# Sparse attention into two MLPs on one core: two batches divide P ahead of its transposing and multiply with V of both heads as the stationary operand

## The chip, the core and the metric

The kernel runs on one core of a Trainium2 chip. The metric is the device time of one execution in microseconds (us). Engines: PE (TensorE), DVE (VectorE), ACT (ScalarE), POOL (GpSimd), and SP, which here only issues DMAs. Each engine works through its own queue in program order; semaphores tie the queues together.

## The reference

Attention over 4 batches, 8 heads, 576 positions and 64 dimensions in float32. The first four heads see the last 32 positions (local), the last four see the earlier positions with the same remainder by 32 (strided). Then two MLPs of 2304 tokens, each 512 to 2048 to 512 with a squared relu.

```python
scores = np.where(masks, scale * (q @ k.T), -1e9)
attn = np.exp(scores - scores.max(-1))
attn = attn / (attn.sum(-1) + 1e-09)
x = (attn @ v)                       # heads side by side: 2304 x 512
for w_in, w_out in ((moe_w_in, moe_w_out), (moe2_w_in, moe2_w_out)):
    h = np.maximum(x @ w_in, 0.0)
    x = (h * h) @ w_out
```

## The kernel before

**The MLPs.** Weights and activations are split into a high and a low fp32r part, and each product is three matmuls. Layer 0 runs over five blocks of tokens (512, 512, 512, 256, 512), each block in steps of 128 hidden rows. In step s the program issues mm1(s+1) (12 matmuls into ps_h; L704), then a relu and a square on ACT (r L744, gh L752) and two DVE products (sq L753, gl L754) on its result, then mm2(s) (12 matmuls into ps_y; L757).

**The attention.** x, the input of layer 0, comes from attention in 48 fills, 12 for each batch. A fill takes two heads u: three local ones for u = 0 (96 queries and 128 keys in each of two groups), three for u = 1, then three strided ones for each u (blocks of 126 in two groups, of 108 in two groups, of 108 in one). Fills are numbered 0 to 47; batch 3 has 24 to 35, batch 4 has 36 to 47. Batches 1 and 2 have their own orders (`ALONE`, `SHARED`), and batches 3 and 4 the order `BETWEEN` (L625).

**A fill in batches 3 and 4.** split_qk (L325: ACT and DVE split queries and keys, and SP loads the next ones), scores_first and scores_second (L351, a head each), mask_first and mask_second (L379, L381: mask and minimum on DVE), exponent (L484, four ACT instructions, in place in s), turn_p (L491, PE transposes of P into ps_pt), keep_p (L499, ACT copies it to pt), values (L507: P is stationary, V with a column of ones moves, so that the sum of P comes out as column 65), divide (L538, L539, L541: DVE adds 1e-9, takes the reciprocal and multiplies into xn), turn_x (L553, PE transposes of xn into ps_x), keep_x (L592, ACT writes the high part of x) and rest_x (L596, DVE writes the low part).

**The order.** `BETWEEN` has ten slots. An entry (function, back) in round n works on fill n - back; all slots are laid end to end in one list `att`. The MLP calls point() after each three matmuls, eight points a step; points 1 to 3 lie inside mm1, point 4 behind it and behind the issue of r, gh, sq and gl, points 5 to 7 inside mm2, point 8 behind it. At each point `att_to` issues as many slots as are due: batch 3 is spread evenly over points 8 of step 15 to 4 of step 30 (116 points), batch 4 over the same stretch 16 steps on. Values are not issued at once: they are put in a list `small`, of which one comes out behind each MLP matmul; divide, in the same slot, issues all that are left.

**Buffers.** The PSUM ring ps_a has three banks, which scores, ps_pt, ps_o and ps_x of batches 3 and 4 take in turn. ps_h has one bank. s, m, pt and den have two buffers each, v has five.

Of the kernel before, what the change touches and what calls it, by code (L numbers as in the profile page):

```python
# [9 lines left out]
F32 = mybir.dt.float32  # L10
F32R = mybir.dt.float32r
I32 = mybir.dt.int32
AF = mybir.ActivationFunctionType
ALU = mybir.AluOpType
AX = mybir.AxisListType

P = 128
B, H, S, D = 4, 8, 576, 64
STRIDE = 32
NPOS = S // STRIDE  # L20
# [6 lines left out]
BLOCKS = [  # L27
    [(0, TB), (TB, TB), (2 * TB, TB), (3 * TB, TB // 2), (NT - TB, TB)],
    [(0, TB // 2)] + [(n * TB + TB // 2, TB) for n in range(4)],
]  # L30
# [21 lines left out]
FIRST_2 = 2  # L52


SFILLS = [(0, 7, 2), (14, 6, 2), (26, 6, 1)]
LQ, LK = 2 * QB, 2 * QB + STRIDE
# [28 lines left out]
def pack_local(q, k, v):  # L85


    qk = np.zeros((B, 2, 3, P, 2 * LQ + LK), np.float32)
    ov = np.ones((B, 2, 3, P, 2, 2, D + 1), np.float32)
    kp = np.zeros((B, 4, STRIDE + S, D), np.float32)  # L90
    vp = np.zeros((B, 4, STRIDE + S, D), np.float32)
    kp[:, :, STRIDE:] = k[:, :4]
    vp[:, :, STRIDE:] = v[:, :4]
    for u in range(2):
        for f in range(3):
            for h in range(2):
                n, rows = 2 * u + h, slice(h * D, (h + 1) * D)
                qk[:, u, f, rows, h * LQ:(h + 1) * LQ] = q[:, n, f * LQ:(f + 1) * LQ].transpose(0, 2, 1)
                qk[:, u, f, rows, 2 * LQ:] = kp[:, n, f * LQ:f * LQ + LK].transpose(0, 2, 1)
                for g in range(2):  # L100
                    k0 = f * LQ + g * QB
                    ov[:, u, f, :, h, g, :D] = vp[:, n, k0:k0 + P]
    return qk, ov.reshape(B, 2, 3, P, VW)


def pack_strided(q, k, v, fill):

    r0, n, ng = fill
    m = n * NPOS
    w = ng * m  # L110
    qk = np.zeros((B, 2, P, 3 * w), np.float32)
    ov = np.ones((B, 2, P, 2, ng, D + 1), np.float32)

    def rows_of(x):
        x = x[:, 4:].reshape(B, 4, NPOS, STRIDE, D)[:, :, :, r0:r0 + n * ng]
        return x.transpose(0, 1, 3, 2, 4).reshape(B, 4, w, D)

    qq, kk, vv = rows_of(q), rows_of(k), rows_of(v)
    for u in range(2):
        for h in range(2):  # L120
            rows = slice(h * D, (h + 1) * D)
            qk[:, u, rows, h * w:(h + 1) * w] = qq[:, 2 * u + h].transpose(0, 2, 1)
            qk[:, u, rows, 2 * w:] = kk[:, 2 * u + h].transpose(0, 2, 1)
            for g in range(ng):
                ov[:, u, :m, h, g, :D] = vv[:, 2 * u + h, g * m:(g + 1) * m]
    return qk, ov.reshape(B, 2, P, 2 * ng * (D + 1))


def both_halves(qk, w, groups):


    rest = qk.shape[-1] - 2 * w
    kw = rest if groups is None else (groups - 1) * (w // groups) + P
    t = np.zeros(qk.shape[:-1] + (2 * w + 2 * kw,), np.float32)
    for h in range(2):
        rows = slice(h * D, (h + 1) * D)
        for half in (slice(0, D), slice(D, P)):
            t[..., half, h * w:(h + 1) * w] = qk[..., rows, h * w:(h + 1) * w]
            k0 = 2 * w + h * kw
            t[..., half, k0:k0 + rest] = qk[..., rows, 2 * w:]  # L140
    return t


def r32(ap):
    return ap.bitcast(F32)
# [3 lines left out]
def tile_attention_then_two_mlps(  # L149
# [9 lines left out]
    nc = tc.nc  # L159
# [6 lines left out]
    apool = ctx.enter_context(tc.tile_pool(name="att", bufs=2))  # L166
# [128 lines left out]
    fills = []  # L295
# [7 lines left out]
    SPLIT = FIRST_2 * PER_B  # L303
    kin, vin = {}, {}
    n_in, n_vin = [0], [0]

    def src_of(i):
        b, u, kind, f = fills[i]
        arrays, at = (loc, (u, f)) if kind == "l" else (st[f], (u,))
        qk0, qk, v = arrays  # L310
        return (qk0[(b,) + at] if b < FIRST_2 else qk[(b - FIRST_2,) + at]), v[(b,) + at]

    def load_qk():
        i = n_in[0]
        if i >= NFILL:
            return
        n_in[0] += 1
        qk = src_of(i)[0]
        tag = "qk" + str(i % 3 if i < SPLIT else 0)
        kin[i] = fpool.tile([P, QK_COLS[tag]], F32, tag=tag, name="qk", bufs=1)  # L320
        nc.sync.dma_start(out=kin[i][:, :qk.shape[-1]], in_=qk)
# [76 lines left out]
    def load_v():  # L398
        i = n_vin[0]
        if i >= NFILL:  # L400
            return
        n_vin[0] += 1
        _, v = src_of(i)
        vin[i] = vfpool.tile([P, VW], F32, tag="v", name="v", bufs=5)
        nc.sync.dma_start(out=vin[i][:, :v.shape[-1]], in_=v)
# [6 lines left out]
    def x_at(n):  # L412

        return 0 if n == TB else 48

    def x_tiles(j):
        if j not in xh:
            xh[j], xl[j] = (x_tile(t, j % 3) for t in ("xh", "xl"))
        return xh[j], xl[j]

    def geometry(i):

        b, u, kind, f = fills[i]
        if kind == "l":
            return QB, P, 2, QB
        r0, n, ng = SFILLS[f]
        m = n * NPOS
        return m, m, ng, m

    def ps_tile(i, name):  # L430

        n_ps[0] += 1
        if fills[i][0] == 0 and n_ps[0] % 7 < KC:
            return ps_y.tile([P, 512], F32, tag=f"y{n_ps[0] % 7}", name=name)
        return ps_a.tile([P, 512], F32, tag="a", name=name)

    n_ps = [0]
    s_ps, s_sb, mx, pt_ps, pt_sb, o_ps, xn, x_ps = ({} for _ in range(8))
    W = D + 1

# [38 lines left out]
    def exponent(i):  # L479
        nq, nk, ng, _ = geometry(i)  # L480
        s, m = s_sb[i], mx.pop(i)
        for j in range(2 * ng):
            blk = s[:nq, j * nk:(j + 1) * nk]
            nc.scalar.activation(out=blk, in_=blk, func=AF.Exp, scale=-1.0, bias=m[:nq, j:j + 1])  # L484

    def turn_p(i):
        nq, nk, ng, _ = geometry(i)
        s = s_sb.pop(i)
        ps = pt_ps[i] = ps_tile(i, "ps_pt")
        for j in range(2 * ng):  # L490
            nc.tensor.transpose(  # L491
                ps[:nk, j * nq:(j + 1) * nq], s[:nq, j * nk:(j + 1) * nk], ident[:nq, :nq]
            )
# [65 lines left out]
    def x_parts(i):  # L559

        b, u, kind, f = fills[i]
        ps = x_ps[i]
        parts = []
        if kind == "l":
            c = u
            t0, t1 = b * S + f * LQ, b * S + (f + 1) * LQ
            for j, (b0, nb) in enumerate(BLOCKS[0]):
                lo, hi = max(t0, b0), min(t1, b0 + nb)
                if lo < hi:
                    parts.append((j, ps[:, lo - t0:hi - t0], lambda x, a=lo - b0, e=hi - b0, o=x_at(nb): x[:, c, o + a:o + e]))  # L570
        else:
            c = 2 + u
            r0, n, ng = SFILLS[f]
            n *= ng
            src = ps[:, :n * NPOS].rearrange("p (r i) -> p i r", i=NPOS)
            i0 = b * NPOS
            for j, (b0, nb) in enumerate(BLOCKS[0]):
                o, nt = x_at(nb), nb
                b0, nb = b0 // STRIDE, nb // STRIDE
                lo, hi = max(i0, b0), min(i0 + NPOS, b0 + nb)  # L580
                if lo < hi:
                    parts.append((
                        j,
                        src[:, lo - i0:hi - i0],
                        lambda x, a=lo - b0, e=hi - b0, o=o, nt=nt: x[:, c, o:o + nt].rearrange(
                            "p (i r) -> p i r", r=STRIDE)[:, a:e, r0:r0 + n],
                    ))
        return parts

    def keep_x(i):  # L590
        for j, src, place in x_parts(i):
            nc.scalar.activation(out=place(x_tiles(j)[0]), in_=src, func=AF.Copy)  # L592

    def rest_x(i):
        for j, src, place in x_parts(i):
            nc.vector.tensor_tensor(  # L596
                out=place(xl[j]), in0=src, in1=place(r32(xh[j])), op=ALU.subtract
            )
        x_ps.pop(i)
# [5 lines left out]
        [],  # L605
        [(scores, 0), (keep_p, 2)],
        [(exponent, 1)],
        [(turn_x, 3), (mask_and_max, 0)],
        [(values, 2), (keep_x, 3)],
# [17 lines left out]
        [(turn_p, 1)],  # L627
        [(keep_p, 1)],
        [(scores_second, 0), (mask_second, 0)],
        [(split_qk, -1)],  # L630
        [(turn_x, 2)],
        [(keep_x, 2)],
        [(rest_x, 2), (exponent, 0)],
        [(values, 1), (divide, 1)],
        [],
    ]
    att = []
# [358 lines left out]
    for k, s in first.items():  # L996

        s, lag, each = (first[NB], 2, 1) if k == NB + 1 else (s - 12, 3, 2)
# [7 lines left out]
    with tc.manual_schedule():  # L1006
# [3 lines left out]
        ps = ps_h.tile([P, TB], F32, tag="h", name="ps_w")[:, :P]  # L1010
# [18 lines left out]
        for s in range(len(steps)):  # L1029
            k, f = steps[s]  # L1030
            layer, j = blocks[k]
# [68 lines left out]
```

## Time and profile before

| | us |
|---|---|
| median of 3 runs | 895.09 |
| lowest and highest | 894.54, 895.76 |
| the profiled execution, its own time | 896.05 |
| span of the profiled execution, first to last instruction | 894.2 |
| PE busy | 872.8 (98%) |
| weight loads (PEld), beside PE | 763.6 (85%) |
| DVE busy | 631.2 (71%) |
| ACT busy | 491.6 (55%) |

Busy times of PE are modelled and overlap; a busy PE is not PE at its peak. The chain of waits, which follows the last instruction back to what released it, gives PE 81% of the span and DVE 13%. An fp32 product shows as two PE instructions, a transpose and an fp32r matmul as one.

### The profile page before, as it was taken

Reading aid. Unit: us, or ns where it says so; the run is one execution under the profiler, and the core shown is the slowest. Engines: PE = TensorE matmul, PEld = TensorE weight load, DVE = VectorE, ACT = ScalarE, POOL = GpSimd, SP = SyncE. Lnnn points to the kernel's source line nnn. Section 1 sums busy time; section 2 is a strip of 40 time slices with the busy share of each in tenths; the row PEclk is TensorE's granted clock in tenths of the full one; section 3 lists DMA queues with packets and bytes.
Section 4 is the critical chain, followed back from the end, with each engine's and each line's share of the span. In section 5 each row is a group of like instructions: output and inputs, shape, how many; then the busy total and the mean of one; then the engine's idle time right before and its main releaser. Section 6 shows DMA issues by size and latency. Waiting matters only on the chain.

```text
span 894.2 us, 14165 instructions
## 1 busy us (share of the span) xinstructions
PE 872.8 (98%) x5289; PEld 763.6 (85%) x5289; DVE 631.2 (71%) x1521; ACT 491.6 (55%) x987; POOL 0.2 (0%) x4
## 2 busy tenths in 40 slices
PE   9699999999999999999999999999999999999997
PEld 8578878888888888899888898899989989998996
DVE  5999983477765666322299996777787787778676
ACT  6787863455555454232377885555545545554443
POOL 0000000000000000000000000000000000000000
PEclk9799999999999999999999999999999999999999
DMA  8966610222223210010566530100020020001001
GB/s 260 321 208 220 200 48 19 69 92 71 70 77 98 79 51 25 1 48 1 183 205 201 165 131 12 48 12 13 9 64 24 1 72 1 24 2 48 1 1 48
DMA packets 45940, 72.02 MB, mean 81 GB/s; under 512 B 3504, under 2 KB 32304, under 8 KB 45872
## 3 DMA queue, kind: packets, MB, share of 16 engines
q1 hardware_dynamic: 45872, 71.12, 24.4%
q8 instruction: 42, 0.69, 0.3%
q14 instruction: 26, 0.21, 0.1%
HBM read 61.67 MB, written 9.44 MB: 80 GB/s over the span
## 4 chain that ended last, share of the span: by engine, by line
PE 81%; DVE 13%; issue 2%; ACT 2%; DMA 1%; SPq 0%; DVEq 0%; ACTq 0%
PE ps_h L696 39%; PE ps_y L696 21%; PE ps_y L919 15%; PE ps_o L507 2%; DVE raw L223 2%; DVE val L234 2%; DVE w L268 2%; PE ps_pt L491 1%; DVE o L939 1%; PE ps_s L351 1%; DVE raw L220 1%; DVE s L468 1%; DVE gl L754 1%; DMA qk<-st_qk_d 1%; PE ps_s L448 1%
## 5 line engine op out<-in xcount | busy, mean ns | idle before, releaser
L696 PE MATMUL ps_h<-xh,w 128*128 128x512 f32 (+1 forms) x1343 | 401.7, 365 | 0.0
L696 PEld LDWEIGHTS ps_h<-xh,w 128*128 128x128 f32 x1343 | 245.4, 189 | 39.0
L696 PE MATMUL ps_h<-xl,w 128*128 128x512 f32 (+1 forms) x640 | 236.3, 369 | 0.0
L696 PE MATMUL ps_y<-gh,w 128*128 128x512 f32 (+1 forms) x640 | 157.3, 376 | 0.0
L696 PEld LDWEIGHTS ps_h<-xl,w 128*128 128x128 f32 x640 | 121.1, 189 | 14.9
L696 PEld LDWEIGHTS ps_y<-gh,w 128*128 128x128 f32 x640 | 107.9, 188 | 16.4
L744 ACT ACTIVATE r<-ps_h 128x512 f32<-128x512 f32 x80 | 47.8, 597 | 121.2 <-PE ps_h L696 84.7
L753 DVE TENSOR_TENSOR sq<-r 128x512 f32<-128x512 f32 x50 | 34.6, 692 | 101.6 <-ACT r L744 101.6
L861 DVE TENSOR_TENSOR xl<-wf,xh 128x768 fp32r<-128x768 f32 (+1 forms) x80 | 79.9, 1009 | 16.2 <-ACT xh L860 15.9
L696 PE MATMUL ps_y<-gl,w 128*128 128x512 f32 (+1 forms) x324 | 85.4, 371 | 0.0
L738 DVE TENSOR_TENSOR sq<-sq 128x512 f32<-128x512 f32 x64 | 44.1, 689 | 53.4 <-ACT sq L737 53.4
L860 ACT ACTIVATE xh<-wf 128x768 fp32r<-128x768 f32 (+1 forms) x80 | 68.9, 880 | 23.3 <-PE ps_y L919 23.3
L737 ACT ACTIVATE sq<-ps_h 128x512 f32<-128x512 f32 x64 | 37.8, 591 | 72.5 <-PE ps_h L696 69.3
L919 PE MATMUL ps_y<-xl,gbh 128*128 128x256 f32 x256 | 71.3, 278 | 0.9 <-DVE xl L861 0.9
L919 PE MATMUL ps_y<-xh,gbl 128*128 128x256 f32 x256 | 71.0, 277 | 0.2 <-DVE gbl L861 0.2
L919 PE MATMUL ps_y<-xh,gbh 128*128 128x256 f32 x256 | 71.1, 278 | 0.0
L754 DVE TENSOR_TENSOR gl<-sq,gh 128x512 fp32r<-128x512 f32 x80 | 55.2, 691 | 21.2 <-ACT gh L750 15.3
L696 PEld LDWEIGHTS ps_y<-gl,w 128*128 128x128 f32 x324 | 55.3, 188 | 8.7
L484 ACT ACTIVATE s<-s,m 96x128 f32<-96x128 f32 (+2 forms) x176 | 55.7, 388 | 5.2 <-DVE m L468 4.8
L919 PE MATMUL ps_y<-xh,gah 128*128 128x256 f32 x192 | 53.7, 280 | 0.0
L919 PE MATMUL ps_y<-xl,gah 128*128 128x256 f32 x192 | 53.3, 278 | 0.2 <-DVE xl L861 0.2
L919 PE MATMUL ps_y<-xh,gal 128*128 128x256 f32 x192 | 53.2, 277 | 0.2 <-DVE gal L880 0.2
(77 smaller groups left out, 1346.4 us busy)
## 6 DMA issues: line engine op xcount, KB each, us to landing
raw<-moe_w_in_d SPq DMA_DIRECT2D x32, 512.0 KB, 4.7
raw<-moe_w_out_d SPq DMA_DIRECT2D x32, 512.0 KB, 4.2
qk<-loc_qk_d SPq DMA_DIRECT2D x12, 416.0 KB, 3.1
out_d<-o SPq DMA_DIRECT2D x18, 256.0 KB, 2.4
y_dram<-o SPq DMA_DIRECT2D x16, 256.0 KB, 2.1
y_in<-y_dram SPq DMA_DIRECT2D x16, 256.0 KB, 3.0
qk<-loc_qk_d SPq DMA_DIRECT2D x12, 304.0 KB, 3.9
v<-loc_v_d SPq DMA_DIRECT2D x24, 130.0 KB, 2.7
```

The source lines that it names most:

```text
L223: nc.vector.scalar_tensor_tensor(out=lower, in0=upper, scalar=-(2 ** 31), in1=lower, op0=ALU.bitwise_and, op1=ALU.bitwise_or)
L234: nc.vector.scalar_tensor_tensor(out=val[n].bitcast(I32), in0=upper, scalar=3, in1=lower, op0=ALU.logical_shift_left, op1=ALU.bitwise_or,)
L484: nc.scalar.activation(out=blk, in_=blk, func=AF.Exp, scale=-1.0, bias=m[:nq, j:j + 1])
L696: nc.tensor.matmul(y[:, c:c + w], lhsT=lhsT, rhs=rhs[:, c:c + w], start=start and c == 0, stop=stop and c + w == n,)
L737: nc.scalar.activation(out=t, in_=ps, func=AF.Relu, scale=W_BACK)
L738: nc.vector.tensor_tensor(out=t, in0=t, in1=t, op=ALU.mult)
L744: nc.scalar.activation(out=r, in_=ps, func=AF.Relu, scale=W_BACK)
L753: nc.vector.tensor_tensor(out=sq, in0=r, in1=r, op=ALU.mult)
L754: nc.vector.tensor_tensor(out=lo, in0=sq, in1=r32(h), op=ALU.subtract)
L860: nc.scalar.activation(out=hi, in_=src, func=AF.Copy)
L861: nc.vector.tensor_tensor(out=lo, in0=src, in1=r32(hi), op=ALU.subtract)
L919: nc.tensor.matmul(y[:, t * HALF:(t + 1) * HALF], lhsT=a[:, i, rows], rhs=w[:, cols], start=first and t == 0 and m == 0, stop=end and t == ...
```

## The change

For batches 3 and 4 the order within a fill and three of its steps are new.

- The exponents also put out their sums (`accum_out`), into den.
- DVE divides P in s by the sums, ahead of turn_p, with one product over the whole of s.
- V is packed on the host with both heads side by side for each group (64 + 64 columns, without ones). values_of_both has V of a group as the stationary operand (128 columns) and the transposed P of both heads as the moving one (192, 252 or 216 columns), and writes x, transposed, for both heads; of each head's result half of the partitions is meant. It is issued at once, not through `small`. turn_x and divide are gone.
- keep_x and rest_x take each head's part with an instruction of its own, on 64 partitions.
- values_of_both stands in slot 4, behind split_qk; keep_x in slot 5, rest_x in 6 (a round earlier than before), the exponents in 7, the division in 8.

```diff
+    def exponent_and_sums(i):
+        nq, nk, ng, _ = geometry(i)
+        s, m = s_sb[i], mx.pop(i)
+        d = dens[i] = apool.tile([P, 4], F32, tag="den", name="den")
+        for j in range(2 * ng):
+            blk = s[:nq, j * nk:(j + 1) * nk]
+            nc.scalar.activation(
+                out=blk, in_=blk, func=AF.Exp, scale=-1.0, bias=m[:nq, j:j + 1],
+                accum_out=d[:nq, j:j + 1],
+            )
+
+    def divide_p(i):
+        nq, nk, ng, _ = geometry(i)
+        d = dens.pop(i)[:nq, :2 * ng]
+        nc.vector.tensor_scalar_add(out=d, in0=d, scalar1=1e-9)
+        nc.vector.reciprocal(out=d, in_=d)
+        s = s_sb[i][:nq, :2 * ng * nk].rearrange("q (j k) -> q j k", j=2 * ng)
+        nc.vector.tensor_tensor(
+            out=s, in0=s, in1=d.unsqueeze(2).to_broadcast([nq, 2 * ng, nk]), op=ALU.mult
+        )
+
+    def values_of_both(i):
+        nq, nk, ng, _ = geometry(i)
+        pt = pt_sb.pop(i)[:nk, :2 * ng * nq].rearrange("k (h g q) -> k h g q", h=2, g=ng)
+        v = vin.pop(i)
+        ps = x_ps[i] = ps_tile(i, "ps_x")
+        for g in range(ng):
+            nc.tensor.matmul(
+                ps[:, 2 * g * nq:2 * (g + 1) * nq],
+                lhsT=v[:nk, g * P:(g + 1) * P],
+                rhs=pt[:, :, g],
+                start=True,
+                stop=True,
+            )
+        load_v()
+
+    def x_parts_of_both(i):
...
     def keep_x(i):
-        for j, src, place in x_parts(i):
+        for j, src, place in (x_parts if i < SPLIT else x_parts_of_both)(i):
             nc.scalar.activation(out=place(x_tiles(j)[0]), in_=src, func=AF.Copy)
 
     def rest_x(i):
-        for j, src, place in x_parts(i):
+        for j, src, place in (x_parts if i < SPLIT else x_parts_of_both)(i):
...
         [(turn_p, 1)],
         [(keep_p, 1)],
         [(scores_second, 0), (mask_second, 0)],
-        [(split_qk, -1)],
-        [(turn_x, 2)],
-        [(keep_x, 2)],
-        [(rest_x, 2), (exponent, 0)],
-        [(values, 1), (divide, 1)],
+        [(split_qk, -1), (values_of_both, 1)],
+        [(keep_x, 1)],
+        [(rest_x, 1)],
+        [(exponent_and_sums, 0)],
+        [(divide_p, 0)],
         [],
```

## Rows read from the trace of the kernel before

**Rows 1.** Windows, batches 3 and 4: stretch, busy time by engine, granted clock, DMA share.

```profile
171.00:373.00 202.00, 201.75 (x1094) 167.06 (x1093) 129.00 (x436) 102.55 (x256) 0.00 (x0) 1.00 0.21 65
```

**Rows 2.** Chain of waits, shares by line, of 171 to 267 and of 277 to 366.

```profile
by line: PE ps_h L696 35.9%; PE ps_y L696 35.5%; PE ps_o L507 8.0%; PE ps_s L351 6.9%; PE ps_pt L491 4.7%; issue 4.4%; PE ps_x L553 2.1%; DVE sq L753 0.7%; DVE gl L754 0.7%; DVE k L337 0.7%; ACT r L744 0.6%; DVE qs L334 0.6%; DVE s L379 0.4
...
by line: PE ps_y L696 41.0%; PE ps_h L696 40.2%; PE ps_o L507 7.9%; PE ps_s L351 4.8%; PE ps_pt L491 4.1%; PE ps_x L553 2.1%
```

**Rows 3.** Chain of waits, pieces of a local round: start us, us, what.

```profile
197.07 0.65 PE ps_o L507 x8
197.72 0.75 PE ps_y L696 x3
...
201.17 0.24 PE ps_s L351 x2
201.40 0.70 PE ps_h L696 x3
...
202.78 0.17 PE ps_x L553 x2
...
205.77 0.37 PE ps_s L351 x2
...
206.84 0.33 PE ps_pt L491 x4
```

**Rows 4.** Chain of waits, values of strided fills (126, 108, 108 in one group).

```profile
226.12 0.83 PE ps_o L507 x8
...
254.19 0.72 PE ps_o L507 x8
...
261.38 0.34 PE ps_o L507 x4
```

**Rows 5.** Timeline of PE: start us, us, engine, line, operation, partitions x columns.

```profile
204.21 0.81 PE L507 MATMUL ps_o<-v,pt 128*96 128x65 f32 x8
...
91.58 1.03 PE L448 MATMUL ps_s<-qk 128*96 128x128 f32 x8
```

**Rows 6.** Groups by line, 171 to 373 us: busy us, mean ns | idle before.

```profile
L381 DVE DVE_READ_ACCUMULATOR2_ANT m<- 96x1 f32 x48 | 3.8, 79 | 0.0
...
L592 ACT ACTIVATE xh<-ps_x 128x24 fp32r<-128x24 f32 x2 | 0.4, 184 | 1.6 <-PE ps_x L553 1.6
```

**Rows 7.** Timeline of DVE in the round of rows 3.

```profile
202.82 0.69 DVE L753 TENSOR_TENSOR sq<-r 128x512 f32<-128x512 f32 x1 [0.41 <-ACT r L744]
203.61 0.69 DVE L754 TENSOR_TENSOR gl<-sq,gh 128x512 fp32r<-128x512 f32 x1
...
205.73 0.15 DVE L538 TENSOR_SCALAR den<-ps_o 96x4 f32<-96x4 f32 x1
205.92 0.17 DVE L539 RECIPROCAL den<-den 96x4 f32<-96x4 f32 x1
206.12 0.42 DVE L541 TENSOR_TENSOR xn<-ps_o,den 96x256 f32<-96x256 f32 x1
```

**Rows 8.** Timeline of ACT in the same round.

```profile
202.19 0.60 ACT L744 ACTIVATE r<-ps_h 128x512 f32<-128x512 f32 x1 [1.92 <-DVE m L381]
202.81 0.63 ACT L752 ACTIVATE gh<-r 128x512 fp32r<-128x512 f32 x1
...
204.23 0.31 ACT L592 ACTIVATE xh<-ps_x 128x192 fp32r<-128x192 f32 x1
204.44 1.27 ACT L484 ACTIVATE s<-s,m 96x128 f32<-96x128 f32 x4
207.21 0.49 ACT L499 ACTIVATE pt<-ps_pt 128x384 f32<-128x384 f32 x1 [1.49 <-PE ps_pt L491]
```

**Rows 9.** Timeline of ACT around the exponents of fill 36.

```profile
260.79 0.60 ACT L744 ACTIVATE r<-ps_h 128x512 f32<-128x512 f32 x1 [1.04 <-issue]
...
261.95 1.27 ACT L484 ACTIVATE s<-s,m 96x128 f32<-96x128 f32 x4
```

**Rows 10.** Chain of waits there: the start of mm2 and turn_p of fill 36.

```profile
260.70 0.68 PE ps_y L696 x3
...
263.43 0.50 PE ps_pt L491 x4
```

More of the change, by code (lines that the diff above doesn't have):

```diff
@@ L141, in both_halves, with heads_together @@
     return t
+def heads_together(v, groups):
+    v = v.reshape(v.shape[:-1] + (2, groups, D + 1))[..., :D]
+    return np.ascontiguousarray(v.swapaxes(-3, -2)).reshape(v.shape[:-3] + (groups * P,))
 def r32(ap):
@@ L309, in src_of @@
         arrays, at = (loc, (u, f)) if kind == "l" else (st[f], (u,))
-        qk0, qk, v = arrays
-        return (qk0[(b,) + at] if b < FIRST_2 else qk[(b - FIRST_2,) + at]), v[(b,) + at]
+        qk0, qk, v0, v = arrays
+        if b < FIRST_2:
+            return qk0[(b,) + at], v0[(b,) + at]
+        return qk[(b - FIRST_2,) + at], v[(b - FIRST_2,) + at]
     def load_qk():
@@ L435, in ps_tile @@
         return ps_a.tile([P, 512], F32, tag="a", name=name)
-    n_ps = [0]
+    n_ps, dens = [0], {}
     s_ps, s_sb, mx, pt_ps, pt_sb, o_ps, xn, x_ps = ({} for _ in range(8))
@@ new lines, in x_parts_of_both @@
+    def x_parts_of_both(i):
+        b, u, kind, f = fills[i]
+        nq, nk, ng, _ = geometry(i)
+        parts = []
+        for h in range(2):
+            rows = slice(h * D, (h + 1) * D)
+            ps = x_ps[i][rows, :2 * ng * nq].rearrange("p (g h q) -> p h g q", g=ng, h=2)[:, h]
+            if kind == "l":
+                for j, (b0, nb) in enumerate(BLOCKS[0]):
+                    o = x_at(nb)
+                    t0 = b * S + f * LQ
+                    if b0 <= t0 and t0 + LQ <= b0 + nb:
+                        a = o + t0 - b0
+                        parts.append((j, ps, lambda x, r=rows, a=a: x[r, u, a:a + LQ].rearrange(
+                            "p (g q) -> p g q", g=ng)))
+                        continue
+                    for g in range(ng):
+                        t1 = t0 + g * nq
+                        lo, hi = max(t1, b0), min(t1 + nq, b0 + nb)
+                        if lo < hi:
+                            parts.append((
+                                j, ps[:, g, lo - t1:hi - t1],
+                                lambda x, r=rows, a=o + lo - b0, e=o + hi - b0: x[r, u, a:e],
+                            ))
+                continue
+            r0, n, _ = SFILLS[f]
+            src = ps.rearrange("p g (r i) -> p g i r", i=NPOS)
+            i0 = b * NPOS
+            for j, (b0, nb) in enumerate(BLOCKS[0]):
+                o, nt = x_at(nb), nb
+                b0, nb = b0 // STRIDE, nb // STRIDE
+                lo, hi = max(i0, b0), min(i0 + NPOS, b0 + nb)
+                if lo < hi:
+                    parts.append((
+                        j, src[:, :, lo - i0:hi - i0],
+                        lambda x, r=rows, a=lo - b0, e=hi - b0, o=o, nt=nt: x[r, 2 + u, o:o + nt].rearrange(
+                            "p (i r) -> p i r", r=STRIDE)[:, a:e, r0:r0 + n * ng].rearrange(
+                            "p i (g r) -> p g i r", g=ng),
+                    ))
+        return parts
@@ L1073 @@
     arrays = {"consts": const_table()}
-    for name, w, groups, (qk, vals) in [("loc", LQ, None, pack_local(q, k, v))] + [
-        (f"st{i}", fill[1] * fill[2] * NPOS, fill[2], pack_strided(q, k, v, fill))
+    for name, w, groups, ng, (qk, vals) in [("loc", LQ, None, 2, pack_local(q, k, v))] + [
+        (f"st{i}", fill[1] * fill[2] * NPOS, fill[2], fill[2], pack_strided(q, k, v, fill))
         for i, fill in enumerate(SFILLS)
@@ L1079 @@
         arrays[name + "_qk"] = both_halves(qk[FIRST_2:], w, groups)
-        arrays[name + "_v"] = vals
+        arrays[name + "_v0"] = vals[:FIRST_2]
+        arrays[name + "_v"] = heads_together(vals[FIRST_2:], ng)
     for n in ("moe_w_in", "moe_w_out", "moe2_w_in", "moe2_w_out"):
@@ L1091 @@
             aps["consts"],
-            [aps["loc" + n] for n in ("_qk0", "_qk", "_v")],
-            [[aps[f"st{i}" + n] for n in ("_qk0", "_qk", "_v")] for i in range(len(SFILLS))],
+            [aps["loc" + n] for n in ("_qk0", "_qk", "_v0", "_v")],
+            [[aps[f"st{i}" + n] for n in ("_qk0", "_qk", "_v0", "_v")] for i in range(len(SFILLS))],
             [aps["moe_w_in"].bitcast(I32), aps["moe2_w_in"].bitcast(I32)],
```

## The prediction, made before the change was run

> **What bounds the kernel now.** I read the windows first, then the chain of waits, then the timelines of ACT and DVE around one fill. The stretch that the change touches is batches 3 and 4, 171 to 373 us. There TensorE is busy 201.75 of 202.00 us at the full granted clock, DVE 129.00 and ACT 102.55 [rows 1]. The chain of waits runs through PE almost alone: in both parts the shares of DVE and ACT lines are under 1% each, and "issue" is 4.4% in the first only, at its start [rows 2]. So two things count: PE work that goes is time won, and a PE instruction that has to wait is time lost, whatever DVE and ACT do meanwhile.
>
> The attention is spread over the matmuls by points. A step s has 12 matmuls of mm1(s+1), then relu and squares, then 12 of mm2(s); points 1 to 3 lie inside mm1, point 4 right behind the relu, 5 to 8 inside and behind mm2. From point to point PE needs 0.70 us (three matmuls) plus what attention puts there [rows 3]. From the due formula with the new list I worked out at which point each slot falls. Batch 3 has 150 slots in 116 points before and 139 after; batch 4 has 120 both times. Between exp(i) in slot 7 and turn_p(i), four slots later, lie 3 or 4 points, so 2.34 or 3.04 us with one scores_first (0.24 us) [rows 3].
>
> **Part 1: PE work removed.** turn_x goes: 44 transposes. In the chain they hold 2.1% of 96 us and 2.1% of 89 us [rows 2], 3.9 us, with the few outside 4.0; one local pair is 0.17 us [rows 3]. All of it lies on PE, the bounding engine: **-4.0 us**.
>
> **Part 2: values.** Before, a local fill has 8 instructions (4 fp32 products, two each) with 96 stationary and 65 moving columns: 0.65 us [rows 3]; strided ones 0.83, 0.72 and 0.34 [rows 4]. After, there are half as many, with 128 stationary columns and 192, 252 or 216 moving ones. No row has that shape. The nearest: eight instructions with 96 stationary columns last 0.81 us with 65 moving columns and 1.03 with 128 [rows 5]. The difference is 0.22/8 = 0.028 us each, so at 128 moving columns one costs 0.081 + 0.028 = 0.109 us, 0.85 ns a column. By that 192 columns take 0.163 us, four of them 0.65; 252 give 0.86; 216 give 0.73 and, with one group, 0.37. That is 0.00 to +0.03 a fill: I take **0**. Bounds: +0.7 us (0.03 for 24 fills), or -1.5 us if the 0.05 us that the three matmuls behind a block of values take longer now (0.75 against 0.70 [rows 3]) goes.
>
> The Trainium skill, TensorE: Matmul & The Clock Gate, LDWEIGHTS, has a load of weights take its columns divided by 1.2 ns: 80 ns for 96, where 0.65/8 = 81 ns stands here, so the trace agrees that the old values were set by their loads. By that rule alone four loads of 128 columns would take 0.43 us for 0.65. The rows speak against taking it alone: at the same 96 stationary columns more moving ones cost more. It is part of the third rival.
>
> **Part 3: what is put between exp and turn_p.** Before, turn_p waits for the exponents. Now it waits for exponents, their sums and the division. The sums: what reading an accumulator costs on ACT no row shows. The nearest are DVE's reading of its own (79 ns) and the shortest ACT instructions (184 ns) [rows 6]. The exponents themselves stay the same four instructions, so a gain is excluded. I take 0.1 us each, near the first row: 0.4 for four; ends 0 and 0.75. The division: add and reciprocal take 0.39 us till the third instruction starts (205.73 to 206.12); a product over 512 elements takes 0.69 and over 256 takes 0.42 [rows 7]. So it lasts 1.08 us for a local fill, 1.07 for 504, 0.99 for 432 and 0.77 for 216 elements, with 0.1 for two handovers.
>
> Without disturbance there is room. Let values(i-1) start at 0. They end at 0.65; two keep_x end by 1.2 (0.21 us start to start [rows 8]), exponents by 1.2 + 1.27 + 0.4 = 2.9, the division by 4.1. turn_p(i) comes 5 to 7 points later, at 4.4 to 5.8. Extra ACT work (keep_x twice, sums) and DVE work (rest_x twice, a product twice as long) then costs nothing. In the old order the cover was as small: exp of fill 28 ends at 205.71 [rows 8] and turn_p runs at 206.84 [rows 3].
>
> But ACT and DVE run in program order, and once in 8 points the relu comes in between. Let m be the end of mm1. r starts at m + 0.09 (260.70, 260.79) and exponents behind r and gh start 1.16 later [rows 9, 10]; gl on DVE ends 2.11 after r's start [rows 7, 8]. Three cases in the new order:
>
> **ACT case**, relu and gh ahead of exp(i): the division is through at m + 1.25 + 1.27 + 0.4 + 0.06 + 1.08 + 0.05 = m + 4.1 (3.95 for 108 rows, 3.0 for one group, +0.47 where keep_x is behind the relu too). turn_p comes 3, 3, 4, 4 and 5 points behind m for fills 34, 35, 38, 43 and 39, at 2.33, 2.34, 3.04, 3.04 and 3.74. Stalls 1.6, 0.65, 1.05, 0.9, 0.8: 5.0 us. Before, the same place was only just covered: exponents end at 263.22 and turn_p runs at 263.43 [rows 9, 10]. There the old order even had values (0.34 us here) in between; they now lie ahead.
>
> **DVE case**, sq and gl between rest_x and the division: DVE is free at m + 2.24, the division through at m + 3.3 (31), 3.05 (32, 47), 3.35 (33). turn_p is due at m + 1.64 (31, 32: two points), 2.33 (33), 2.1 (47). Stalls 1.65, 1.4, 1.0, 0.95: 5.0 us.
>
> **keep_p case**: values now follow keep_p by two slots, not six. With relu and gh ahead of keep_p (fills 40, 45) it ends at m + 0.09 + 1.16 + 0.49 + 0.05 = m + 1.8, while values are due at m + 1.4: 0.4 each, 0.8 us.
>
> Together **+10.8 us**, 9.0 with sums that cost nothing and 12.4 with 0.19 us each.
>
> **Part 4: the rest.** Behind the waiting division stands mask_first(i+1) on DVE; its bank is needed again only by values(i) four slots later, so no further wait. Behind keep_x, which waits for values, stands exp on ACT, counted above. A fill takes 4 banks of the three-deep ring for 5. v loads leave four slots earlier on SP, into five buffers, and nobody waits. scores_first sometimes waits for split_qk behind the relu (0.37 for 0.24 [rows 3]; four such in batch 3): in the new order those fills have 6 points for it, **-0.5 us**.
>
> **Sum.** 896.05 (profiled execution; its span of 894.2 and 1.85 around it) - 4.0 + 10.8 - 0.5 = 902.35. The median of the runs is 0.96 below the profiled one: **901.4 us**. With the bounds of parts 2 and 3: 898.1 to 903.7; a point more or less at some fills moves a stall by 0.7, so 897.5 to 905.
>
> **Rivals.**
> Faster: the cover holds. ACT and DVE reach the division of the hit fills before turn_p, because the relu finds them ahead. For it: DVE is busy only 129 and ACT 103 of 202 us [rows 1], and most fills have about 1 us to spare. Against it: 0.2 us to spare at the fill of [rows 10]. Point from which it decides: the nine stalls of turn_p together under 2.7 us. Then 896.05 - 4.0 - 0.5 - 0.96 = 890.6, up to 893.3.
>
> Worse: the sums are long, 0.2 us each and no overlap between exponents (+0.1 each), and in batch 3 also the undisturbed fills with 5 points (4.4 us, needing 4.1 + 0.8) wait. Then 12.4 + 4 x 0.5 + 2 more, 16 in all: 907.
>
> Near no change: half of the stalls, as when only the DVE case holds (5.0), 895.6; or the price of values is set by the columns of their loads alone: 0.081 x 128/96 = 0.108 us each [rows 3], four 0.43, 0.22 less a fill, 5 us: 896.4.
>
> **Chances.** Forecast 0.70, faster 0.13, near no change 0.10, worse 0.07. About 0.2% (1.8 us) is what a measurement of this kernel tells from no change. Faster 0.14, same 0.10, slower 0.76. The range takes in the no-change rival and the worse one and leaves out the faster: 893.5 to 907.
>
> **What would show it.** After: no ps_x transposes by an identity; values about 0.65 us per local fill in the chain; waits of turn_p's weight loads for the division's product, some nine of 0.6 to 1.7 us, at fills whose relu lies between points of slot 5 and slot 8; two small waits of values for keep_p. PE's chain in 171 to 373 us then has some 10 us of DVE and ACT pieces. If turn_p hardly waits, part 3 is wrong and the kernel is faster; if values cost 0.45 us, part 2 is; if every fill waits, the sums are mis-sized.

## The result, and the profile after

| | us |
|---|---|
| median of the runs, changed kernel | 908.14 (907.89 to 908.72) |
| median of the runs, kernel before, on the same chip | 895.11 |
| ratio | 1.0145, 95% interval 1.0129 to 1.0160 |
| profiled execution, its span | 908.21, 906.3 |
| forecast, range | 901.4, 893.5 to 907.0 |

The change costs 13.0 us. The sign and the mechanism were forecast; the forecast loss was 6.3 us. The busy times of the changed kernel's page:

```profile
PE 868.4 (96%) x5157; PEld 758.0 (84%) x5157; DVE 649.1 (72%) x1563; ACT 511.4 (56%) x1117; POOL 0.2 (0%) x4
```

PE has 4 us less to do and the kernel takes 13 us longer, so PE waits. The windows row of the same stretch as [rows 1] (length, then busy time of PE, PEld, DVE, ACT, POOL, clock, DMA) says where:

```profile
171.00:373.00 202.00, 187.75 (x907) 153.60 (x906) 141.03 (x459) 117.74 (x371) 0.00 (x0) 0.99 0.20 65
```

PE is idle 14.25 of 202 us, where it was idle 0.25. DVE and ACT have 12 and 15 us more to do and are still at 70% and 58%. The list of waits of PE from 171 to 385 us (who waited for whom, total us, times, longest) names turn_p in nearly all of it:

```profile
PE ps_pt L580 <- DVE s L514: 12.5, 11, 1.8
PE ps_pt L580 <- ACT gh L841: 2.3, 1, 2.3
PE ps_x L524 <- ACT pt L588: 0.4, 2, 0.3
```

L580 is turn_p, L514 the division's product, L524 values of both, L588 keep_p. For the kernel before the same list is empty. The timeline of PE gives each of them (in brackets the idle time ahead, and its releaser):

```profile
231.33 0.55 PE L580 MATMUL ps_pt<-cst,s 108*108 108x108 f32 x4 [1.80 <-DVE s L514]
239.95 0.37 PE L580 MATMUL ps_pt<-cst,s 108*108 108x108 f32 x2 [1.46 <-DVE s L514]
248.67 0.62 PE L580 MATMUL ps_pt<-cst,s 126*126 126x126 f32 x4 [1.28 <-DVE s L514]
257.86 0.55 PE L580 MATMUL ps_pt<-cst,s 108*108 108x108 f32 x4 [1.84 <-DVE s L514]
265.79 0.37 PE L580 MATMUL ps_pt<-cst,s 108*108 108x108 f32 x2 [0.78 <-DVE s L514]
283.74 0.52 PE L580 MATMUL ps_pt<-cst,s 96*128 96x96 f32 x4 [2.34 <-ACT gh L841]
303.49 0.52 PE L580 MATMUL ps_pt<-cst,s 96*128 96x96 f32 x4 [1.18 <-DVE s L514]
312.56 0.52 PE L580 MATMUL ps_pt<-cst,s 96*128 96x96 f32 x4 [1.18 <-DVE s L514]
321.40 0.52 PE L580 MATMUL ps_pt<-cst,s 96*128 96x96 f32 x4 [0.24 <-DVE s L514]
324.42 0.76 PE L524 MATMUL ps_x<-pt,v 128*128 128x192 f32 x3 [0.15 <-ACT pt L588]
347.83 0.55 PE L580 MATMUL ps_pt<-cst,s 108*108 108x108 f32 x4 [1.16 <-DVE s L514]
364.29 0.62 PE L580 MATMUL ps_pt<-cst,s 126*126 126x126 f32 x4 [0.58 <-DVE s L514]
367.49 1.12 PE L524 MATMUL ps_x<-pt,v 126*128 126x252 f32 x4 [0.26 <-ACT pt L588]
382.65 0.37 PE L580 MATMUL ps_pt<-cst,s 108*108 108x108 f32 x2 [1.02 <-DVE s L514]
```

By their order and shapes the waits of turn_p are fills 31, 32, 33, 34, 35, then 36, 38, 39, 40, 43, 45 and 47. All nine that the forecast named are there, and three more: 36, 40 and 45. The fills with the relu elsewhere wait for nothing.

One of the DVE cases, fill 31, shows how the time goes: the squares (L842, L843) stand between the relu and the division's three instructions (L511, L512, L514). Timelines of ACT, DVE, PE and its weight loads:

```profile
228.12 0.60 ACT L833 ACTIVATE r<-ps_h 128x512 f32<-128x512 f32 x1 [0.31 <-PE ps_h L785]
...
228.75 0.69 DVE L842 TENSOR_TENSOR sq<-r 128x512 f32<-128x512 f32 x1 [1.52 <-ACT r L833]
229.55 0.69 DVE L843 TENSOR_TENSOR gl<-sq,gh 128x512 fp32r<-128x512 f32 x1
230.16 0.16 DVE L511 TENSOR_SCALAR den<-den 108x4 f32<-108x4 f32 x1
230.36 0.18 DVE L512 RECIPROCAL den<-den 108x4 f32<-108x4 f32 x1
230.57 0.61 DVE L514 TENSOR_TENSOR s<-s,den 108x432 f32<-108x432 f32 x1
...
227.86 0.84 PE L785 MATMUL ps_y<-gh,w 128*128 128x512 f32 x3
228.55 0.28 PE L359 MATMUL ps_s<-k,qs 128*108 128x256 f32 x1
228.66 0.87 PE L785 MATMUL ps_y<-gh,w 128*128 128x512 f32 x3
...
231.29 0.37 PEld L580 LDWEIGHTS ps_pt<-cst,s 108*108 108x108 f32 x4 [2.21 <-issue]
```

DVE waits 1.52 us for r, then needs 2.43 us until P is divided at 231.18. PE has six matmuls and one product of scores_first to do meanwhile and is through at 229.53.

The chain of waits of the changed kernel can't be set beside [rows 2 to 4]: it breaks off at 319 us, and its shares add up to 65% of the span.

### The profile page after: what moved, and what is told of

The parts are those of the page before. It is cut to its first block, busy times and chain, and to the rows that moved or that the text cites. A ratio compares the mean times of both kernels' runs of the same rounds, so it can differ in the third digit from the quotient of the medians.

```text
span 906.3 us, 14042 instructions
## 1 busy us (share of the span) xinstructions
PE 868.4 (96%) x5157; PEld 758.0 (84%) x5157; DVE 649.1 (72%) x1563; ACT 511.4 (56%) x1117; POOL 0.2 (0%) x4
## 4 chain that ended last, share of the span: by engine, by line
PE 57%; DVE 4%; ACT 2%; issue 2%; DVEq 0%; ACTq 0%
PE ps_h L785 29%; PE ps_y L1008 15%; PE ps_y L785 12%; DVE o L1028 1%; PE ps_x L524 1%; DVE xl L950 0%; DVE gbl L950 0%; ACT s L503 0%; ACT sq L826 0%; ACT r L833 0%; PE ps_pt L580 0%; DVE sq L827 0%; ACT gah L967 0%; DVE gal L950 0%; DVE s L966 0%
## 5 line engine op out<-in xcount | busy, mean ns | idle before, releaser
L842 DVE TENSOR_TENSOR sq<-r 128x512 f32<-128x512 f32 x50 | 34.6, 692 | 96.3 <-ACT r L833 96.3
L843 DVE TENSOR_TENSOR gl<-sq,gh 128x512 fp32r<-128x512 f32 x80 | 55.2, 691 | 20.7 <-ACT gh L839 14.6
L235 ACT ACTIVATE raw<-raw 128x512 f32<-128x512 f32 x64 | 43.3, 676 | 13.0 <-DVE raw L229 12.9
```

What stands on the lines that cost most here:

```text
L235: nc.scalar.activation(out=upper, in_=upper, func=AF.Copy, scale=2.0 ** (W_EXP // 8 - 112))
L842: nc.vector.tensor_tensor(out=sq, in0=r, in1=r, op=ALU.mult)
L843: nc.vector.tensor_tensor(out=lo, in0=sq, in1=r32(h), op=ALU.subtract)
```

## The experiments

The theory: the whole loss is PE waiting at turn_p (and twice at values) because of where the division stands in the queues; without the waits the change wins time. The rivals: values with more moving columns, or the amount of work on ACT and DVE, cost more than counted. Beside the runs of each experiment the kernel before measured 894.8 to 895.2 us, so times of different experiments compare within some 0.4 us.

**Without the division.**

```diff
-                accum_out=d[:nq, j:j + 1],
...
-        [(divide_p, 0)],
+        [],
```

> The changed kernel without the sums and without the division of P (P stays undivided, so x is not scaled); all else, the slots too, is as in the changed kernel. Theory (the whole loss is TensorE waiting: 13.2 us in the nine forecast fills and some 4.4 in fills 36, 40 and 45, against 4.5 us won): turn_p waits for the exponents only. The DVE case goes (fills 31, 32, 33, 47), of the ACT case 0.5 us is left at fill 34, fill 36 keeps about 1 us behind the block's stores, values behind keep_p keep 0.75. About 2.2 of 17.6 us of stalls left: 908.1 - 15.4 = 892.7 us, 891.5 to 894. Rival (values with 192 to 252 moving columns, or the doubled keep_x and rest_x, cost more than counted): all of that is still here, so above 900 us.

Measured: 889.71 us, ratio 0.9939 (0.9922 to 0.9955). No wait of a PE matmul at turn_p is left; values behind keep_p keep their 0.4. So all that the change adds besides, twice the keep_x and rest_x and the wider products, costs nothing that shows; without the division the kernel is 5.2 us faster than before. I had expected 3 us more: I left 2.2 us of stalls, where the list has 0.4 of idle time, and took the gain as 4.5.

**Without the sums.**

```diff
-        d = dens[i] = apool.tile([P, 4], F32, tag="den", name="den")
+        dens[i] = ones
...
-                accum_out=d[:nq, j:j + 1],
```

> The changed kernel with the division, but by a tile of ones: the exponents put out no sums (so x is not scaled), DVE's three instructions stay in their place. The sums took 0.38 us a fill on ACT in the trace (1.65 against 1.27 us for four exponents). Theory: they lengthen only the stalls with the exponents on the way (34, 38, 39, 43, 36, 40, 45 and half of it at 35): 7.5 x 0.38 = 2.9 us less, 905.3 us. Rival (the sums delay ACT's whole queue, relu included, so that every fill pays): 24 x 0.38 = 9 us less, 899. Other rival (they are hidden): 908.

Measured: 901.86 us, ratio 1.0074 (1.0059 to 1.0089): 6.3 us less than the changed kernel, not 2.9. The experiment took away more than the sums. DVE's add and reciprocal no longer wait for the exponents; at fill 34 they run while these are still going on. Timelines of DVE and ACT:

```profile
254.90 0.16 DVE L511 TENSOR_SCALAR ones<-ones 108x4 f32<-108x4 f32 x1
255.10 0.18 DVE L512 RECIPROCAL ones<-ones 108x4 f32<-108x4 f32 x1
255.38 0.61 DVE L514 TENSOR_TENSOR s<-s,ones 108x432 f32<-108x432 f32 x1
...
254.03 1.20 ACT L504 ACTIVATE s<-s,m 108x108 f32<-108x108 f32 x4
```

So 0.38 us of sums and 0.39 us of add and reciprocal go where exponents are on the way: the idle time ahead of turn_p falls from 1.84 to 1.17 at fill 34, from 1.18 to 0.44 and 0.47 at 38 and 39, from 1.16 to 0.49 at 43. In the DVE case it stays (1.80 and 1.79 at fill 31, 1.46 and 1.46 at 32, 1.02 and 1.02 at 47). Two fills change sides. At fill 35, forecast as an ACT case, it rises from 0.78 to 0.85: there gl ends after the exponents, so the squares hold the division. At fill 33, a DVE case, it falls from 1.28 to 1.07: in the changed kernel the last sum ended at 245.38 and held r back to 245.40, 0.47 us behind the start of mm2, and here it is 0.26; there the rival (the sums delay the relu) is right, by 0.21 us. At fill 45 it stays as well (0.58 and 0.62): DVE's own queue holds the division (next section). In all, the idle time of PE falls from 15.2 to 11.3 us. Of the other 2.4 us, 1.7 fit the slow clock behind fill 36, which this run doesn't have (its wait there is 1.57 us; last section). The share of the sums alone this run can't give.

**Two slots more in batch 3.**

```diff
+    att_end[2] += 2
     n_att = [0]
```

> The changed kernel, with the two slots that follow batch 3's last one (exponents and division of fill 36) still issued in batch 3's stretch: 141 slots in its 116 points, 118 instead of 120 in batch 4's. Theory (the exponents of fill 36 stand on ACT behind the four stores at the end of the token block, which wait for their DMAs; they were ahead of them in the kernel before): the 2.5 us at fill 36 go, other fills move by at most a point: 905.6 us, 904 to 907. Rival (turn_p of fill 36 waits for gh, as the profile's releaser says): 908.

Measured: 896.50 us, ratio 1.0015 (1.0006 to 1.0024): 11.6 us less than the changed kernel, with the same work. I had expected 2.5. From 181 to 275 us PE waits for nothing: with 141 slots instead of 139 the relu falls behind the division in all the fills 25 to 35. I had written "other fills move by at most a point" as if a point were nothing. Idle time of 5.9 us is left, mostly in batch 4, and for each wait some 0.17 us of refilling (below).

**Fill 36 alone.** What holds it in the changed kernel, timeline of ACT:

```profile
276.95 1.07 ACT L894 ACTIVATE o<-ps_y 128x512 f32<-128x512 f32 x2
279.67 1.25 ACT L894 ACTIVATE o<-ps_y 128x512 f32<-128x512 f32 x2 [1.66 <-DMA y_dram<-o]
280.82 0.39 ACT L503 ACTIVATE s<-s,m 96x128 f32<-96x128 f32 x1
```

L894 copies the finished token block out; the third copy waits for the first one's DMA. The exponents of fill 36 stand behind them. In the kernel before they were due 21 points earlier, ahead of the block's end, since batch 3's stretch then held eleven slots more.

```diff
+                if at == spans[1][1] + 1:
+                    att_to(att_end[2] + 2)
```

> The changed kernel with its own spacing of the slots (139 in batch 3's 116 points, 120 in batch 4's), but the exponents and the division of fill 36 issued at the one point behind batch 3's stretch, ahead of the block's four stores, and not 12 points later behind them. No other slot moves. Theory (ACT waits in the stores for their DMAs, and the exponents of fill 36 stand behind them): the 2.5 us at fill 36 go and nothing else, 905.6 us, 905 to 906.3. Rival (the profile's releaser gh, or a matter of the spacing): 908.

Measured: 904.57 us, ratio 1.0103 (1.0088 to 1.0118): 3.6 us less. The 2.34 us ahead of turn_p of fill 36 are gone and the other eleven waits of turn_p stay within 0.02 us. The 1.1 us beyond the expected 2.5 fit the clock: the changed kernel lost 1.7 us of full speed behind that wait (last section), and here every stretch of 10 us from 170 to 400 us has a granted clock of 1.00. The releaser gh that the profile named was not the cause: gh ended at 283.60, the division's product at 283.59, and turn_p started 0.15 us later.

**The relu, one point apart.** Two kernels in which all fills of batch 3 meet the relu at the same place; they differ in the start of the stretch by one point.

```diff
+    att_end[2] += 6
...
+    spans[1] = tuple(p + 2 for p in spans[1])
```

> The changed kernel with 145 slots in batch 3's 116 points (six of batch 4's come earlier), so that ten slots are eight points and each fill of batch 3 meets the relu at the same place; the stretch starts two points later, which puts the relu one point behind the division in fills 24 to 36. Theory (a fill stalls only where relu, squares and division meet): no wait of turn_p in batch 3; batch 4 keeps some 4 us (37, 38, 40, 41, 44): 890.6 + 4 = 894.6 us, 893 to 897. Rival (the amount of ACT and DVE work in batch 3 is too much for the place): waits all over batch 3, above 900.

```diff
-    spans[1] = tuple(p + 2 for p in spans[1])
+    spans[1] = tuple(p + 3 for p in spans[1])
```

> As the kernel with 145 slots, but the stretch starts three points later, not two: all slots of batch 3 come 0.7 us later against the matmuls, and the relu falls between exponents and division in fills 25 to 36. Nothing else differs. Theory: each of these 12 fills stalls as fill 31 did in the changed kernel (1.9 us; 1.6 for the two with one group): 22 us more than the kernel with two points, 916 to 917. Rival (one point matters little, the waits come from the amount of work): within 4 us of it.

Measured: 896.41 us (ratio 1.0014, 1.0005 to 1.0023) and 927.75 us (ratio 1.0364, 1.0339 to 1.0389). With the relu behind the division batch 3 has no wait until this one, at fill 37, whose exponents now stand behind the block's copies and the next relu:

```profile
280.20 0.88 PE L580 MATMUL ps_pt<-cst,s 96*128 96x96 f32 x4 [2.68 <-DVE s L514]
```

With the relu between exponents and division every fill from 24 to 36 waits, two of them here:

```profile
211.07 0.52 PE L580 MATMUL ps_pt<-cst,s 96*128 96x96 f32 x4 [1.75 <-DVE s L514]
221.64 0.52 PE L580 MATMUL ps_pt<-cst,s 96*128 96x96 f32 x4 [1.74 <-DVE s L514]
```

The work and its rate are the same in both; 0.7 us of place makes 31 us. Of these, 22 were expected; the list of waits holds 27.0 us of idle time for 4.7. That leaves 9 us for refilling after 13 more waits and for the clock (last section). The rival of too much work is out.

**turn_p late.**

```diff
         [(scores_first, 0), (mask_first, 0)],
-        [(turn_p, 1)],
-        [(keep_p, 1)],
+        [(keep_x, 2)],
+        [(rest_x, 2)],
         [(scores_second, 0), (mask_second, 0)],
-        [(split_qk, -1), (values_of_both, 1)],
-        [(keep_x, 1)],
-        [(rest_x, 1)],
+        [(split_qk, -1)],
+        [(turn_p, 1)],
+        [(keep_p, 1)],
         [(exponent_and_sums, 0)],
         [(divide_p, 0)],
-        [],
+        [(values_of_both, 1)],
```

> The changed kernel with another order of the same steps: slot 0 scores_first, 1 keep_x (of two fills back), 2 rest_x (two back), 3 scores_second, 4 split_qk, 5 turn_p (one back), 6 keep_p (one back), 7 exponents and sums, 8 division, 9 values of both (one back). The division has seven slots (5 to 7 points) until turn_p, instead of three (2 to 4). Theory (only the place of turn_p costs): no waits at turn_p; the gain of 4.5 us shows: 890.6 us, 889.5 to 892.5, faster than the kernel before. Rival (DVE or ACT have too much work in batch 3, whatever the place): waits of TensorE stay in batch 3, above 897 us.

Measured: 890.10 us, ratio 0.9943 (0.9928 to 0.9957), 18.0 us less than the changed kernel with the same work in another order, and faster than the kernel before. turn_p waits nowhere. That the number came out so near is in part luck: the gain is larger than 4.5 (below), and waits of scores_first take some of it back. Chain of waits in a local round, to set beside [rows 3]:

```profile
203.85 0.65 PE ps_x L524 x4
204.50 0.70 PE ps_h L785 x3
...
208.44 0.33 PE ps_pt L580 x4
```

What is left is in the list of waits: weight loads of scores_first for the split keys.

```profile
PEld ps_s L359 <- DVE k L345: 3.1, 8, 0.9
```

**scores_first a slot later as well.** On top of the order with turn_p late:

```diff
-        [(scores_first, 0), (mask_first, 0)],
         [(keep_x, 2)],
+        [(scores_first, 0), (mask_first, 0)],
         [(rest_x, 2)],
```

> The order with turn_p late (890.1 us), with keep_x in slot 0 and scores_first in slot 1 instead of the other way round. There, scores_first waited for the split of the keys on DVE eight times (3.1 us of idle weight loads). Theory: a point later the split is done, 1.5 to 2.5 us less: 888.1 us, 887.3 to 889. Rival (the mask, now a point later, delays exponents or scores_second as much): 890 or more.

Measured: 889.06 us, ratio 0.9934 (0.9922 to 0.9946), the fastest of the kernels that compute the whole. The waits of scores_first fall from 3.1 to 0.2 us of idle weight loads; one wait of 0.71 us at a turn_p of batch 4 comes up instead, so 1.0 us is won, not 1.5 to 2.5; the intervals of the two runs overlap, so even this is not sure. Pieces of its chain of waits, values of strided fills, to set beside [rows 4]:

```profile
223.89 0.85 PE ps_x L524 x4
...
230.91 0.73 PE ps_x L524 x4
...
237.85 0.37 PE ps_x L524 x2
```

**A product alone, in the kernel before.**

```diff
-        [(values, 1), (divide, 1)],
+        [(product_by_one, 0), (values, 1), (divide, 1)],
```

> The kernel before with one thing added: DVE multiplies P by a tile of ones (same shapes as the division's product, 0.38 to 0.69 us) in slot 8, ahead of values, with turn_p in its old place three slots later. Values still stand between the exponents and turn_p (0.34 to 0.83 us of cover), there are no sums, add or reciprocal. Theory (a division costs what is missing between its end and turn_p's place): the product ends 0.9 us behind the exponents with its handovers; by the distances from exponents to turn_p in the trace of before it is late at fills 27 (0.1), 33 (0.45), 34 (0.1), 36 (0.7), 40 (0.1) and, behind the squares, at 39 and 44 (0.25 each): 1.9 us, 897.0 us, 896.2 to 898.5. Rival (the early division as such makes the loss, wherever values stand): 903 or more. Other rival (DVE has time for it): 895.2.

Measured: 897.10 us, ratio 1.0025 (1.0014 to 1.0035), as expected. PE's idle time lies where the distance from exponents to turn_p was shortest, at fills 33 and 36 (0.27 and 0.68 us). At the other five places forecast (0.1 to 0.25 us each) no PE idle time shows; the two waits are worth some 1.3 of the 2.3 us with refilling, so the number is borne out and its parts only in the main. In the old order a product between exponents and turn_p costs 2 us. The changed kernel put add, reciprocal and sums there too, and took values, 0.34 to 0.83 us of PE work, out of that place.

## Why the prediction was right or wrong

**What bounds it** was right: PE's waits decide, DVE and ACT at 70% and 58% don't.

**Part 1 and 2, the gain**, was too small. The price of values was right to 0.01 us: 0.65 for 0.65 forecast, and in the chain of the order with scores_first later 0.85, 0.73 and 0.37 for 0.86, 0.73 and 0.37. But I took the 0.05 us that the three matmuls behind values used to need in addition [rows 3] as staying. They need 0.70 now (204.50 above), 1.2 us if it holds for all 24 fills; I had it as a bound only, and put 1.5 there where 24 x 0.05 is 1.2. With 4.0 for turn_x and 0.5 to 1 for scores_first (an estimate from its idle weight loads, 2.1 us before and 0.2 in the fastest order) that is 5.7 to 6.2; the fastest order is 6.1 us under the kernel before with a wait of 0.7 still in it. So the gain is 6 to 7 us, not 4.5. The Trainium skill, TensorE: Matmul & The Clock Gate, Back-to-back issue gap, gives the isolated gap from one matmul to the next at the full clock as the columns divided by 2.4, in ns, and 2.5; an estimate by it for 192 columns is 82 ns. Here one instruction took 0.65/4 = 163 ns, twice that; for these fp32 instructions the measurement decides.

**Part 3, the waits**, was right in kind and in nine of its places and too small in size: the term that failed. With a loss of 13.0 and a gain of 6 to 7, the waits are worth 19 to 20 us, where I had 10.8. The gain that was too small took back some 2 us of this miss. The trace gives the waits one by one, as idle time plus 0.17 us each for refilling PE. The 0.17 is an estimate: a transpose that has waited takes 0.25 us to its end (the mean of the local ones is 249 ns), while in an unbroken stream each adds 0.08 (0.33 for four).

| | forecast us | measured us |
|---|---|---|
| nine fills named (31 to 35, 38, 39, 43, 47) | 10.0 | 11.7 + 9 x 0.17 = 13.2 |
| fill 36 | 0 | 2.3 + 0.17 = 2.5 |
| the clock behind it | 0 | 1.7 |
| fills 40, 45: keep_p and, not forecast, turn_p | 0.8 | 1.2 + 4 x 0.17 = 1.9 |
| sum | 10.8 | 19.3 |

- The nine: the arithmetic of the queues held. For fill 31 I had the division through at m + 3.3; r started at 228.12, so m = 228.03, and turn_p's weights were loaded from 231.29, m + 3.26. What failed is the other side, when PE is there. I counted PE's stream from the end of mm1, but the next matmul had started at 227.86, 0.17 us ahead of m, and the one-group fill 32 issues one product in scores_first, not two (0.11 us). With a handover of 0.15 us from product to matmul (0.05 taken), each stall is some 0.35 us longer than forecast, on average (3.2 us over nine).
- Fill 36: I worked from points only and put no wait there. That the block's copies stand in ACT's queue and wait for DMAs is in no term of the prediction; in the old order the exponents of fill 36 were issued 21 points earlier. The experiment for fill 36 shows it.
- Fills 40 and 45: the relu stands ahead of split_qk, and split_qk, keep_x and the exponents follow behind it on ACT. I put only the wait of values for keep_p there (0.8; 0.15 and 0.26 measured, with refilling 0.75). turn_p waited too, 0.24 and 0.58 us. At fill 40 keep_x of the fill before took 0.87 us in six parts, where I had counted two parts in 0.55, and DVE waited 0.35 us for the exponents behind it. At fill 45 DVE worked without a break from sq at 358.74 to the end of the division's product at 364.14: squares, mask_second, split_qk and rest_x, a queue that the prediction has no case for.

**The sums** were sized right: 1.65 us for four exponents with sums, from 196.78 to 198.43, where they took 1.27 [rows 8], so 0.38 for 0.4. The trace shows what they are, a second instruction each, of 0.19 us, of which 0.09 lie ahead of the next exponent:

```profile
196.78 0.40 ACT L503 ACTIVATE s<-s,m 96x128 f32<-96x128 f32 x1
197.09 0.19 ACT L503 ACTIVATION_READ_ACCUMULATOR s<-s,m 96x1 f32 x1
197.18 0.39 ACT L503 ACTIVATE s<-s,m 96x128 f32<-96x128 f32 x1
```

**The rivals.** "Faster: the cover holds" fell in this kernel and stands in the one with turn_p late: 890.1 for 890.6 forecast. "Worse", 907, came nearest to the number, but by another mechanism: the fills with five points and no relu in between don't wait. Values priced by their loads alone fell: 0.65, not 0.43.

**What stays open:** the share of the sums in the waits, which the run without them doesn't separate from add and reciprocal; and the parts of the gain, of which only the values and turn_x are read from rows.

## What to carry to other kernels

When PE is the bound and steps of a side chain are issued between its matmuls, count for each pair of producer and PE consumer the PE time between their places, and set it against the producer's queue at its worst alignment with the periodic work of the same engines, not at its mean load. The new form, P divided ahead of its transposing and V stationary, was worth having (5 to 6 us here), but only with turn_p moved back by more than the length of the added chain; the same work in another order made 908 or 889 us. A list that gets shorter also shifts every later step against fixed events, such as a block's copies that wait for DMAs: look up what stands in the queue at each new place.

## What the runs showed of the hardware that was not expected

A single wait of PE was followed by a fall of its clock. In the changed kernel PE did nothing for 2.34 us ahead of turn_p of fill 36, and 1.3 us after it had started again the granted clock fell to 0.50, which is 1.2 GHz. Stretches of 1 us, columns as above, the clock third from the end:

```profile
282.00:283.00 1.00, 0.00 (x0) 0.00 (x0) 0.44 (x3) 0.97 (x5) 0.00 (x0) 1.00 0.49 186
...
284.00:285.00 1.00, 1.00 (x8) 0.87 (x6) 0.97 (x6) 0.49 (x1) 0.00 (x0) 1.00 0.06 16
285.00:286.00 1.00, 1.00 (x4) 0.69 (x4) 0.88 (x2) 0.00 (x0) 0.00 (x0) 0.50 0.03 8
286.00:287.00 1.00, 1.00 (x5) 0.90 (x4) 0.41 (x1) 0.41 (x1) 0.00 (x0) 0.50 0.00 0
287.00:288.00 1.00, 1.00 (x4) 0.81 (x4) 0.94 (x6) 0.58 (x2) 0.00 (x0) 0.50 0.00 0
288.00:289.00 1.00, 1.00 (x6) 0.96 (x5) 0.76 (x2) 0.13 (x2) 0.00 (x0) 0.79 0.00 0
```

Three stretches at 0.50 and one at 0.79 are 1.7 us of full speed lost, on top of the wait. Where fill 36 alone was moved ahead this wait is gone and the clock stays at 1.00, which points to the wait as the cause (one traced execution of each). The wait of 2.68 us at fill 37, in the kernel with the relu behind the division, was followed by the same: stretches of 1 us at 0.54, 0.50, 0.50 and 0.76 from 280 to 284 us. The other waits of the changed kernel, up to 1.84 us, are in stretches with a granted clock of 1.00.

In the kernel with the relu between exponents and division the waits of 1.74 to 1.76 us in local fills, 9 to 11 us apart, were followed by stretches of 10 us at 0.83 from 180 to 200 and 210 to 240 us. Two of them, at 202.14 and 295.37, were not, nor were the waits of 1.44 to 1.85 us in strided fills; no run shows what parts them. Five such stretches cost 8.5 us, which is most of what the waits of that kernel leave unexplained in the profiled execution (929.83 us). It isn't the same in every execution: the mean granted clock was 0.982 in those of 929.83 and 930.87 us and 0.988 and 0.986 in those of 925.12 and 925.67.
